# First products in blocks of 512 tokens two batches behind the attention, x carried through memory in float32, thirteen float32 pairs instead of nine

## The chip, the cores and the metric

The kernel runs on one core of a Trainium2 chip. The core has a matrix engine (TensorE, called PE in the rows; its weight loads are PEld), VectorE (DVE), ScalarE (ACT), GpSimd (POOL) and SyncE (SP), which here only issues DMAs. The metric is the device time of one execution in microseconds; lower is better. Arrays are prepared on the host before the launch (q and k are transposed, the weights are handed over as pairs of 32-bit words), and everything after that is on the core.

## The reference

Weights are float64 in the input; they reach the kernel as two 32-bit words each and are decoded to float32 on the chip. What is computed, with B = 8 batches, H = 12 heads, S = 448, D = 64, d_model 768, d_ff 1024:

```
scores = (1/sqrt(64)) * q @ k^T - log(448)
attn   = 1 / (1 + exp(-scores))
x      = (attn @ v) as [3584 tokens, 768]
a = x @ w1 ;  b = x @ w2
out = ((a * b) @ w3) @ w_out          # float32
```

## The kernel before

Two heads make a pair: 6 pairs in a batch, 48 in all. A pair is worked in 4 **slots**, one for each chunk of keys (three of 128, one of 64), so there are 192 slots, 24 in a batch. In slot s PE does the scores of that chunk, then the attention product (`av`) of the slot before; between them ACT makes the sigmoids.

There are two kinds of pair. The first `PLAIN` = 9 pairs (slots 0 to 35) are **plain**: float32 matmuls on float32 operands (tiles `qp`, `ap`, `vv`; lines 203 and 255), which cost PE more but need no splitting. The other 39 split each operand into a float32r high part and a rest (`qs`, `kh`, `kl`, `vs`, `ah`, `al`; lines 206, 232 and 262), which costs DVE, ACT and POOL work. The first split pair needs tiles of a pool `pf` that takes the room of the pool `pp` for early weights, so its q and k are loaded at the pair before it (`prepare`, line 399).

A pair's result is 128 columns of x (one of NK = 6 chunks, `kc`) for the 448 tokens of its batch. `combine` (line 267) splits it into `xh` and `xl`, the operands of the **first products**, on ACT and DVE. The first products, `up` (line 330), multiply x by w1 and w2, each product as three float32r matmuls (high by high, high by rest, rest by high): 8 column chunks x 2 weights x 6 chunks x 3 = 288 matmuls for a block of tokens. They go between the slots' scores and `av`, 12 in a slot (`ups`, line 418), one batch behind: the block of batch b-1 goes into the slots of batch b. The blocks take turns at 384 and 512 tokens: an even batch leaves its last 64 tokens (`CARRY`) as split parts in memory (`x_dram`), and the odd batch after it reads them back ahead of its own 448. The seventh block ends after the last slot, and the eighth (512 tokens) is done in the tail. The product a*b (`g`) of each column chunk goes to memory (`g_dram`, line 352).

Weights are decoded by DVE in six instructions for a job (lines 93 to 109), after ACT has made the magnitude (line 86); then ACT casts the high part and DVE subtracts it (lines 73 and 74). w1 and w2 are 16 jobs of 128 x 768, w3 16 jobs of 128 x 512 that go to memory. `starts` and `steps` (lines 366 to 369) say in which slot each step stands: eight w1/w2 jobs in slots 1 to 22, the other eight in slots 25 to 35, while first products already run; the w3 jobs stand in every pair of batches 2, 4 and 6. The first 13 jobs (`EARLY`) have three buffers for the raw words (pool `pp`), the rest one (pool `pd`).

The order on PE and SP is the order in which the code is written (`manual_schedule`, line 362); up to slot 31 the same holds for ACT and POOL. DVE's order, and later ACT's, is chosen by the scheduler. Every engine works its own queue strictly in order.

After the slots comes the tail: the last block of first products with w_out decoded beside it, then w3 times w_out (line 593), then the last product in blocks of two batches (line 626).

Of the kernel before, what the change touches and what calls it, by code (L numbers as in the profile page):

```python
# [11 lines left out]
F32 = mybir.dt.float32  # L12
F32R = mybir.dt.float32r
# [12 lines left out]
def sigmoid_attention_bilinear_ffn(  # L26
# [20 lines left out]
    P = 128  # L47
# [16 lines left out]
    phase_d, phase_s = ExitStack(), ExitStack()  # L64
    pd = phase_d.enter_context(tc.tile_pool(name="pd", bufs=2))
# [3 lines left out]
    x_dram = dram.tile([NK, P, 2, CARRY], F32, name="x_dram")  # L69
# [6 lines left out]
    def load_words(src, pool=None):  # L76
        if pool is None:
            raw = pd.tile([P, NK, P, 2], U32, name="raw", bufs=1)[:, :src.shape[1]]
        else:
            raw = pool.tile([P, *src.shape[1:-1], 2], U32, name="raw")  # L80
        nc.sync.dma_start(out=raw, in_=src)
        return raw

    def magnitude(raw):
        f = pd.tile([P, *raw.shape[1:-1]], F32, name="f")
        nc.scalar.activation(f, raw[..., 1].bitcast(F32), AF.Abs, scale=HW_SCALE)  # L86
        return f
# [29 lines left out]
    px0 = phase_a.enter_context(tc.tile_pool(name="px0", bufs=NK, side="right"))  # L117
    pa = phase_a.enter_context(tc.tile_pool(name="pa", bufs=2, side="right"))
    px = (px0, px1)
# [107 lines left out]
    def short_scores(ks, qs):  # L227


        sp = ps.tile([P, 2, 512], F32, name="sp", bufs=2)[:, :, :S]  # L230
        for j in range(2):
            nc.tensor.matmul(sp[:, j], ks[:, j], qs[:, j], start=True, stop=True)  # L232
        t = pf[0].tile([P, S], F32, name="st", bufs=1)
        add_halves(t, [sp[:, j] for j in range(2)])
        return t
# [31 lines left out]
    def combine(b, kc, accs):  # L267
        if len(accs) == 1:
            src = accs[0][:, :S]
        else:  # L270
            src = pm.tile([P, S], F32, name="t", bufs=1)
            add_halves(src, [acc[:, :S] for acc in accs])
        second = b % 2
        n = BLOCKS[second]
        xh = px[second].tile([P, n], F32R, name="xh")
        xl = px[second].tile([P, n], F32R, name="xl")
        if second:
            for i, x in enumerate((xh, xl)):
                nc.sync.dma_start(out=x[:, :CARRY].bitcast(F32), in_=x_dram[kc, :, i])
            split(xh[:, CARRY:], xl[:, CARRY:], src, nc.scalar.copy, nc.vector)  # L280
        else:
# [24 lines left out]
    def load_job(i):  # L306
        _, _, cs, src = jobs[i]
        raws[i] = load_words(src[:, cs], pp) if i < EARLY else load_words(src[:, cs])

    def decode_weights():  # L310

        for i, (n, at, cs, _) in enumerate(jobs):
            if i + 2 < EARLY:
                load_job(i + 2)
            for k in (i, i + 1):
                if k not in fs and k in raws:
                    fs[k] = magnitude(raws[k])
            f = decode(raws.pop(i), fs.pop(i))
            if i + 1 >= EARLY and i + 1 < len(jobs):
                load_job(i + 1)  # L320
            if n == 3:
                nc.sync.dma_start(out=w3_dram[at, :, cs], in_=f)
                yield
                continue
            yield
            half, at = divmod(at, NH)
            split(wh[n][half][:, at, cs], wl[n][half][:, at, cs], f, nc.scalar.copy, nc.vector)
            yield

    def up(b, xs, banks, pool, bufs):  # L330

        n_t = BLOCKS[b % 2]
        at_t = b // 2 * 2 * S + b % 2 * BLOCKS[0]
        for fc in range(NF):
            for n in (1, 2):
                acc = pool.tile([P, 512], F32, name="up", tag=next(banks), bufs=bufs)
                for kc in range(NK):
                    xh, xl = xs[kc]
                    for m, (w, x) in enumerate(((wh[n], xh), (wh[n], xl), (wl[n], xh))):
                        nc.tensor.matmul(  # L340
                            acc[:, :n_t], w[fc // NH][:, fc % NH, kc], x,
                            start=(kc == 0 and m == 0), stop=(kc == NK - 1 and m == 2),
                        )
                        if (kc, m) != (NK - 1, 2):
                            yield
                if n == 1:
                    a_sb = pm.tile([P, BLOCKS[1]], F32, name="a_sb", bufs=1)[:, :n_t]
                    nc.scalar.copy(out=a_sb, in_=acc[:, :n_t])
                    yield
            g = pm.tile([P, BLOCKS[1]], F32, name="g", bufs=1)[:, :n_t]  # L350
            nc.vector.tensor_tensor(out=g, in0=acc[:, :n_t], in1=a_sb, op=ALU.mult)
            nc.sync.dma_start(out=g_dram[fc, :, at_t:at_t + n_t], in_=g)
            yield

# [10 lines left out]
    first = NPAIR * NC  # L365
    starts = [1 + 3 * i for i in range(8)] + [first + 1 + 3 * i // 2 for i in range(8)]
    assert len(starts) == 2 * NF
    later = [p * NC + 1 for p, (b, _) in enumerate(pairs) if b > 1 and b % 2 == 0][:2 * NF]
    steps = starts + [s + 2 - s // first for s in starts] + later

    EARLY = sum(s < (PLAIN - 1) * NC for s in starts)
    qks, vvs = {}, {}
    for p in range(2):
# [6 lines left out]
    xs = {b: [] for b in range(B)}  # L380
    filler = iter(())
# [4 lines left out]
    def attend_due(slot):  # L386
        while waiting and waiting[0][0] <= slot:
            _, p, c, ops = waiting.pop(0)
            if c == 0:
                accs[p] = [  # L390
                    ps.tile([P, 512], F32, name="av", bufs=2) for _ in range(1 if p < PLAIN else 2)
                ]
            attend(c, ops, vs[p], accs[p])
            if c == NC - 2:
                b, kc = pairs[p]
                xs[b].append(combine(b, kc, accs.pop(p)))
                del vs[p]
# [18 lines left out]

    chunks = [0, NC - 1, *range(1, NC - 1)]
    ups = -(-(NF * 2 * NK * 3) // (NPAIR * NC))
    slot = 0
    for p, (b, hp) in enumerate(pairs):  # L420
# [4 lines left out]
        if p == PLAIN - 1:  # L425
            phase_p.close()
            pf.append(phase_a.enter_context(tc.tile_pool(name="pf", bufs=2, side="right")))
        qs, kh, kl, ks = splits.pop(p)
        for i, c in enumerate(chunks):
            prepare(p, i)  # L430
# [23 lines left out]
    p3 = phase_w.enter_context(tc.tile_pool(name="p3", bufs=2, side="right"))  # L454
    woh = p3.tile([P, NF, DM], F32R, name="woh", bufs=1)
# [10 lines left out]
    filler = up(B - 1, xs[B - 1], itertools.repeat("acc"), ps2, 8)  # L466
    for jc in range(NF):
        take(filler, 10)
        for half in range(2):
            ms = slice(half * NM, (half + 1) * NM)  # L470
            src = w_out[jc * P:(jc + 1) * P].rearrange("p (m u) -> p m u", u=2)[:, ms]
            raw = load_words(src, p3)
            f = decode(raw, magnitude(raw))
            split(woh[:, jc, ms], wol[:, jc, ms], f, nc.scalar.copy, nc.vector)
    ics = [c + NH * h for c in range(NH) for h in range(2)]
    w3s = {0: w3_chunk(0)}
    take(filler, 10 ** 6)
    phase_x.close()
    phase_d.close()
# [228 lines left out]
```

## Time and profile before

| what | value |
|---|---|
| median of 3 runs | 1094.63 us (1092.42 to 1095.91) |
| the profiled execution | 1092.5 us |
| its span, first to last instruction | 1090.3 us |
| mean granted TensorE clock | 0.986 of full speed |
| PE busy | 1054.4 us, 97% |
| DVE busy | 820.0 us, 75% |
| ACT busy | 614.4 us, 56% |
| moved by DMA | 150.69 MB, 138 GB/s on the mean |

The span runs from the first to the last instruction, and the profiled execution took 2.2 us more than its span. Busy shares are means over stages that have different limits, so the table alone does not say what a change is worth: the stages have to be looked at one by one.

### The profile page before, as it was taken

What the parts mean: (1) busy time and instruction counts of PE and PEld (TensorE: products, weight loads), DVE (VectorE), ACT (ScalarE), POOL (GpSimd) and SP (SyncE); (2) the same over time, 40 slices, a digit from 0 to 9 for tenths busy, and PEclk for the clock granted to TensorE, in tenths of its full rate; (3) what the DMA queues carried; (4) which work ended last, traced back from release to release, by engine and by line L of the source; (5) the groups of instructions that cost most, each with busy time, mean ns of one, the idle gap of its engine ahead of it and who ended that gap; (6) DMA issues with size and microseconds to landing.
All of it is one profiled execution on the core that took longest, in us unless ns stands there. A gap on an engine that the chain in (4) does not pass through costs nothing.

```text
span 1090.3 us, 14870 instructions
## 1 busy us (share of the span) xinstructions
PE 1054.4 (97%) x5076; PEld 902.9 (83%) x5076; DVE 820.0 (75%) x1335; ACT 614.4 (56%) x937; POOL 183.6 (17%) x277
## 2 busy tenths in 40 slices
PE   7899689999999999999999999999999999999998
PEld 1245579888899988789998889998889999999997
DVE  6778778788787877887787866867875767868672
ACT  5664557667677766667776667774325442424230
POOL 0001042223332221333322323310000000000000
PEclk9899889999999999999999999999999999999999
DMA  8574444455444444444444443324433735657452
GB/s 247 167 208 118 113 112 114 122 142 144 108 108 121 116 131 133 124 121 116 115 123 116 139 112 104 87 63 127 142 113 109 261 116 200 228 188 223 159 163 76
DMA packets 119002, 150.69 MB, mean 138 GB/s; under 512 B 16336, under 2 KB 104592, under 8 KB 118928
## 3 DMA queue, kind: packets, MB, share of 16 engines
q1 hardware_dynamic: 118928, 149.76, 47.0%
q8 instruction: 40, 0.66, 0.3%
q14 instruction: 34, 0.28, 0.1%
HBM read 118.26 MB, written 31.46 MB: 137 GB/s over the span
## 4 chain that ended last, share of the span: by engine, by line
PE 71%; DVE 14%; DMA 6%; ACT 3%; issue 3%; SPq 2%; POOL 1%; DVEq 0%; ACTq 0%; POOLq 0%
PE up L340 30%; PE up L626 19%; PE av L262 8%; PE sp L206 7%; PE up L593 5%; DMA qq<-qT 2%; DMA raw<-w3T 2%; DVE al L224 2%; DMA raw<-w 1%; DVE raw L106 1%; ACT f L86 1%; DVE f L101 1%; DVE t L194 1%; PE sp L232 1%; DVE w L74 1%
## 5 line engine op out<-in xcount | busy, mean ns | idle before, releaser
L340 PE MATMUL up<-xh,w 128*128 128x384 f32 (+1 forms) x1536 | 466.3, 367 | 0.7 <-issue 0.7
L340 PEld LDWEIGHTS up<-xh,w 128*128 128x128 f32 x1536 | 287.7, 189 | 39.6 <-issue 6.9
L340 PE MATMUL up<-xl,w 128*128 128x384 f32 (+1 forms) x768 | 282.1, 367 | 0.0
L187 ACT ACTIVATE ah<-sp,bias 128x896 fp32r<-128x896 f32 x117 | 117.9, 1008 | 83.1 <-PE sp L206 82.3
L340 PEld LDWEIGHTS up<-xl,w 128*128 128x128 f32 x768 | 145.3, 189 | 15.0
L224 DVE TENSOR_TENSOR al<-sp,ah 128x896 fp32r<-128x896 f32 x117 | 127.4, 1089 | 30.0 <-ACT sp L187 28.3
L74 POOL TENSOR_TENSOR kl<-kk,kh 128x896 fp32r<-128x896 f32 x39 | 83.8, 2148 | 392.1 <-DVE kh L73 350.8
L626 PE MATMUL up<-gs,w 128*128 128x448 f32 x576 | 119.3, 367 | 0.0
L626 PEld LDWEIGHTS up<-gs,w 128*128 128x128 f32 x576 | 108.1, 188 | 9.9
L187 ACT ACTIVATE sp<-sp,bias 128x896 f32<-128x896 f32 x117 | 113.7, 971 | 0.0
L262 PE MATMUL av<-ah,vs 128*128 128x448 f32 x312 | 103.7, 372 | 6.0 <-DVE t L194 3.9
L262 PE MATMUL av<-al,vs 128*128 128x448 f32 x234 | 87.2, 373 | 5.1 <-DVE al L224 4.8
L206 PE MATMUL sp<-qs,kh 128*128 128x448 f32 x234 | 87.4, 374 | 4.5 <-DVE kh L73 4.5
L626 PE MATMUL up<-ga,w 128*128 128x448 f32 x432 | 89.5, 366 | 0.0
L206 PE MATMUL sp<-qs,kl 128*128 128x448 f32 x234 | 87.4, 373 | 1.7 <-POOL kl L74 1.7
L74 POOL TENSOR_TENSOR vs<-vv,vs 128x256 fp32r<-128x256 f32 x78 | 62.5, 814 | 147.4 <-DVE vs L73 144.9
L626 PEld LDWEIGHTS up<-ga,w 128*128 128x128 f32 x432 | 81.1, 188 | 7.1
L246 DVE TENSOR_TENSOR ah<-st,ah 64x448 fp32r<-64x448 f32 x78 | 52.1, 668 | 45.2 <-ACT st L187 43.8
L86 ACT ACTIVATE f<-raw 128x768 f32<-128x768 f32 (+2 forms) x48 | 34.1, 710 | 77.3 <-DMA raw<-w3T 25.0
L262 PEld LDWEIGHTS av<-ah,vs 128*128 128x128 f32 x312 | 58.5, 188 | 16.3 <-issue 8.5
L73 ACT CAST ga<-graw 128x448 fp32r<-128x448 f32 x48 | 25.8, 566 | 70.1 <-DMA graw<-g_dram 70.1
L193 ACT COPY t<-av 64x448 f32<-64x448 f32 x78 | 41.2, 528 | 33.7 <-PE av L262 32.7
(74 smaller groups left out, 1519.8 us busy)
## 6 DMA issues: line engine op xcount, KB each, us to landing
graw<-g_dram SPq DMA_DIRECT2D x72, 448.0 KB, 4.4
qq<-qT SPq DMA_DIRECT2D x78, 224.0 KB, 4.0
kk<-kT SPq DMA_DIRECT2D x78, 224.0 KB, 4.5
raw<-w SPq DMA_DIRECT2D x16, 768.0 KB, 5.7
vv<-vL SPq DMA_DIRECT2D x48, 192.0 KB, 2.6
raw<-w3T SPq DMA_DIRECT2D x16, 512.0 KB, 4.4
g_dram<-g SPq DMA_DIRECT2D x32, 256.0 KB, 2.2
g_dram<-g SPq DMA_DIRECT2D x32, 192.0 KB, 1.9
```

The lines of the kernel that those rows point to most:

```text
L73: hi_engine(out=dst_hi, in_=src)
L74: lo_engine.tensor_tensor(out=dst_lo, in0=src, in1=dst_hi, op=ALU.subtract)
L86: nc.scalar.activation(f, raw[..., 1].bitcast(F32), AF.Abs, scale=HW_SCALE)
L187: nc.scalar.activation(dst, src, AF.Sigmoid, bias=bias[:n], scale=scale)
L193: nc.scalar.copy(out=dst[rows], in_=src[j][others])
L206: nc.tensor.matmul(sp[:, j], k[:, j, at:at + n], qs[:, j], start=m == 0, stop=m == 1)
L224: nc.vector.tensor_tensor(out=al, in0=sp, in1=ah, op=ALU.subtract)
L246: nc.vector.tensor_tensor(out=a[others, j], in0=t[rows], in1=a[rows, j], op=ALU.subtract)
L262: nc.tensor.matmul(accs[j][:, :S], v[:, c, j].rearrange("p u d -> p (u d)"), a[:, j], start=first and m == 0, stop=last and m == len(ops) - 1,
L340: nc.tensor.matmul(acc[:, :n_t], w[fc // NH][:, fc % NH, kc], x, start=(kc == 0 and m == 0), stop=(kc == NK - 1 and m == 2),)
L593: nc.tensor.matmul(acc[:, :NM], a[:, jc], w[:, jc, ms], start=(jc == 0 and m == 0), stop=(jc == NF - 1 and m == 2),)
L626: nc.tensor.matmul(acc[:, :TB], w[:, c, ms], g[:, c], start=(c, m) == (0, 0), stop=(c, m) == (NH - 1, 2),)
```

## The change

- x goes through memory whole, in float32. `combine` leaves a float32 tile `t` (an ACT copy in a plain pair, the sum of two halves in a split one); `store_x` writes it a slot later, `load_x` reads 512 tokens of one chunk two slots after that (`xr`), and `split_x` splits them in the slot after the load.
- First products go in 7 blocks of 512 tokens instead of 8 of 384 and 512, so 2016 matmuls instead of 2304. They begin at slot 53 (`BEGIN`) and no longer at slot 26, with 12 in a slot as before; 60 of them are left after the last slot, and the seventh block is in the tail.
- `PLAIN` is 13: slots 0 to 51 are plain, 35 pairs are split.
- All 16 w1/w2 jobs stand in slots 1 to 45, one in every 2.75 slots, all with three buffers; the magnitude of the next job stands two slots after a job's decoding and the split of its own three slots after. The w3 jobs stand in every second pair from the 14th pair on, with their loads one job ahead.
- Each `g` is stored seven matmuls after it was asked of DVE (`late`), and no longer at once.
- Sixteen matmuls on zeros stand ahead of the first scores.
- The raw words of w_out get a pool of their own in the tail.

```diff
-    CARRY = 64
-    BLOCKS = (S - CARRY, S + CARRY)
-    PLAIN = 9
+    TU = 512
+    NU = NT // TU
+    PLAIN = 2 * NPAIR + 1
...
-    x_dram = dram.tile([NK, P, 2, CARRY], F32, name="x_dram")
+    x_dram = dram.tile([NK, P, NT], F32, name="x_dram")
...
-    px1 = phase_x.enter_context(tc.tile_pool(name="px1", bufs=NK, side="left"))
+    px = phase_x.enter_context(tc.tile_pool(name="px", bufs=2 * NK - 1, side="left"))
...
     def combine(b, kc, accs):
+        t = pa.tile([P, S], F32, name="t")
         if len(accs) == 1:
-            src = accs[0][:, :S]
+            nc.scalar.copy(out=t, in_=accs[0][:, :S])
         else:
-            src = pm.tile([P, S], F32, name="t", bufs=1)
-            add_halves(src, [acc[:, :S] for acc in accs])
-        second = b % 2
-        n = BLOCKS[second]
-        xh = px[second].tile([P, n], F32R, name="xh")
-        xl = px[second].tile([P, n], F32R, name="xl")
-        if second:
-            for i, x in enumerate((xh, xl)):
-                nc.sync.dma_start(out=x[:, :CARRY].bitcast(F32), in_=x_dram[kc, :, i])
-            split(xh[:, CARRY:], xl[:, CARRY:], src, nc.scalar.copy, nc.vector)
-        else:
-            split(xh, xl, src[:, :n], nc.scalar.copy, nc.vector)
-            xt = pm.tile([P, 2, CARRY], F32R, name="xt")
-            split(xt[:, 0], xt[:, 1], src[:, n:], nc.scalar.copy, nc.vector)
-            nc.sync.dma_start(out=x_dram[kc], in_=xt.bitcast(F32))
+            add_halves(t, [acc[:, :S] for acc in accs])
+        return t
+
+    def store_x(b, kc, t):
+        nc.sync.dma_start(out=x_dram[kc, :, b * S:(b + 1) * S], in_=t)
+
+    def load_x(n, kc):
+        xr = pm.tile([P, TU], F32, name="xr")
+        nc.sync.dma_start(out=xr, in_=x_dram[kc, :, n * TU:(n + 1) * TU])
+        return xr
+
+    def split_x(xr):
+        xh = px.tile([P, TU], F32R, name="xh")
+        xl = px.tile([P, TU], F32R, name="xl")
+        split(xh, xl, xr, nc.scalar.copy, nc.vector)
         return xh, xl
...
+                        if late is not None and (n, kc, m) == (1, 2, 0):
+                            nc.sync.dma_start(out=g_dram[late[0], :, at_t:at_t + TU], in_=late[1])
+                            late = None
...
-    starts = [1 + 3 * i for i in range(8)] + [first + 1 + 3 * i // 2 for i in range(8)]
-    later = [p * NC + 1 for p, (b, _) in enumerate(pairs) if b > 1 and b % 2 == 0][:2 * NF]
-    EARLY = sum(s < (PLAIN - 1) * NC for s in starts)
+    starts = [1 + 11 * i // 4 + k for i in range(2 * NF) for k in (0, 2, 3)]
+    later = [p * NC + 1 for p in range(PLAIN + 1, len(pairs), 2)][:2 * NF]
+    EARLY = 2 * NF
+    PER = NPAIR * NC
+    BEGIN = 2 * PER + NC + 1
...
+    warm = ps.tile([P, 512], F32, name="up", tag="up", bufs=2)
+    for _ in range(16):
+        nc.tensor.matmul(warm[:, :S], zeros[:, :P], zeros, start=True, stop=True)
...
-    filler = iter(())
+    filler = itertools.chain(*(up(n, xs[n], itertools.repeat("up"), ps, 2) for n in range(NU - 1)))
...
+    def x_due(slot):
+        for at in [k for k in xts if (k[0] * NPAIR + k[1] + 1) * NC < slot]:
+            store_x(*at, xts.pop(at))
+        for n in range(NU):
+            for kc in range(NK):
+                at = (n + 1) * PER + (kc + 1) * NC + 3
+                if slot == at:
+                    xrs[n, kc] = load_x(n, kc)
+                if slot == at + 1:
+                    xs[n].append(split_x(xrs.pop((n, kc))))
...
-            if b > 0 and (hp, i) == (0, 2):
-                take(filler, 10 ** 6)
-                filler = up(b - 1, xs[b - 1], itertools.repeat("up"), ps, 2)
-            take(filler, ups)
+            x_due(slot)
+            if slot >= BEGIN:
+                take(filler, ups)
...
+    for at in range(slot, slot + NC + 1):
+        x_due(at)
     take(filler, 10 ** 6)
...
-    filler = up(B - 1, xs[B - 1], itertools.repeat("acc"), ps2, 8)
+    filler = up(NU - 1, xs[NU - 1], itertools.repeat("acc"), ps2, 8)
```

How this moves instructions is shown at three places. The first is ACT at the end of the second plain pair, where its order is the written one. Before, `xh` and `xt` are casts of the attention result `av`, and `ap` the sigmoid of a slot:

```order
L187 ACTIVATE ap<-sp,bias 128x896
L73 CAST xh<-av 128x384
L73 CAST xt<-av 128x64
L187 ACTIVATE ap<-sp,bias 64x896
L73 CAST w<-f 128x768
L187 ACTIVATE ap<-sp,bias 128x896
L86 ACTIVATE f<-raw 128x768
```

Now, at the same place, with `t` the float32 copy of the pair's result:

```order
L184 ACTIVATE ap<-sp,bias 128x896 x2
L83 ACTIVATE f<-raw 128x768
L267 COPY t<-av 128x448
L184 ACTIVATE ap<-sp,bias 64x896
L73 CAST w<-f 128x768
L184 ACTIVATE ap<-sp,bias 128x896 x2
```

The two casts, the second of which stands behind a subtraction on DVE, have given way to one copy, and the cast of x is now taken from a reloaded tile in later slots.

The second place is PE at the first split pair. Before, 12 first products (`up`) already stand in each of the slots around it:

```order
L255 MATMUL av<-ap,vv 64x448 x2
L206 MATMUL sp<-qs,kh 128x448
L206 MATMUL sp<-qs,kl 128x448
L206 MATMUL sp<-qs,kh 128x448
L206 MATMUL sp<-qs,kl 128x448
L340 MATMUL up<-xh,w 128x384
L340 MATMUL up<-xl,w 128x384
```

Now the plain slots run up to it bare, and the first products begin one slot later:

```order
L252 MATMUL av<-ap,vv 64x448 x2
L203 MATMUL sp<-qs,kh 128x448
L203 MATMUL sp<-qs,kl 128x448
L203 MATMUL sp<-qs,kh 128x448
L203 MATMUL sp<-qs,kl 128x448
L252 MATMUL av<-ap,vv 64x448 x2
L229 MATMUL sp<-qs,ks 128x448 x2
L347 MATMUL up<-xh,w 128x512
L347 MATMUL up<-xl,w 128x512
```

So the whole of slots 0 to 52 has no first products beside it.

The third place is the queue of SP in a pair among the split ones. Before, the stores of `g` and of the carried tokens `xt` stand right behind the work that makes them:

```order
L352 DMA g_dram<-g 128x512
L285 DMA x_dram<-xt 128x128
L151 DMA vv<-vL 128x3x128
L155 DMA vv<-vL 64x128 x2
L81 DMA raw<-w3T 128x4x256
L322 DMA w_dram<-f 128x512
L142 DMA qq<-qT 64x2x448 x2
L142 DMA kk<-kT 64x2x448 x2
```

Now, for a pair of the same kind:

```order
L273 DMA x_dram<-t 128x448
L139 DMA qq<-qT 64x2x448 x2
L139 DMA kk<-kT 64x2x448 x2
L277 DMA xr<-x_dram 128x512
L352 DMA g_dram<-g 128x512
L148 DMA vv<-vL 128x3x128
L152 DMA vv<-vL 64x128 x2
```

Each pair has gained a store of 224 KB and a load of 256 KB, the loads of q and k stand between the two, and the store of `g` has moved behind them.

## Rows read from the trace of the kernel before

**Rows 1.** Part 1 of the page: busy us (share of the span) xinstructions.

```profile
PE 1054.4 (97%) x5076; PEld 902.9 (83%) x5076; DVE 820.0 (75%) x1335; ACT 614.4 (56%) x937; POOL 183.6 (17%) x277
```

**Rows 2.** Four stages: us; busy PE, PEld, DVE, ACT, POOL (count); PEclk; DMA; GB/s.

```profile
0.00:66.30 66.30, 55.38 (x205) 13.66 (x205) 47.68 (x71) 41.72 (x55) 0.20 (x4) 0.92 0.68 211
66.30:162.00 95.70, 81.12 (x374) 60.48 (x373) 74.21 (x105) 47.60 (x65) 16.47 (x22) 0.91 0.47 126
162.00:746.40 584.40, 578.95 (x2822) 519.10 (x2821) 458.19 (x708) 410.80 (x602) 166.95 (x252) 1.00 0.43 116
746.40:1090.30 343.90, 338.91 (x1680) 309.64 (x1680) 239.92 (x452) 114.32 (x216) 0.00 (x0) 1.00 0.51 166
```

**Rows 3.** PE in order of time, early: start us, us, instruction [idle before <-releaser].

```profile
4.17 3.55 PE L203 MATMUL sp<-qp 64*128 64x448 f32 x8 [4.17 <-DMA qp<-kT]
...
29.45 1.02 PE L203 MATMUL sp<-qp 64*128 64x448 f32 x4
...
31.30 1.02 PE L203 MATMUL sp<-qp 64*128 64x448 f32 x4
...
40.32 1.76 PE L255 MATMUL av<-ap,vv 64*64 64x448 f32 x4 [2.48 <-ACT ap L187]
...
83.66 1.02 PE L203 MATMUL sp<-qp 64*128 64x448 f32 x4
...
87.83 1.02 PE L203 MATMUL sp<-qp 64*128 64x448 f32 x4
```

**Rows 4.** ACT in order of time, two places; columns as in rows 3.

```profile
39.16 0.21 ACT L73 CAST xt<-av 128x64 fp32r<-128x64 f32 x1 [2.82 <-DVE xl L74]
...
118.70 0.89 ACT L86 ACTIVATE f<-raw 128x768 f32<-128x768 f32 x1 [3.38 <-DMA raw<-w]
```

**Rows 5.** The chain that ended last: start us, us, what.

```profile
512.34 2.12 PE up L340 x12
...
526.58 2.12 PE up L340 x12
...
587.34 2.75 PE up L340 x12
...
604.12 2.75 PE up L340 x12
...
746.38 65.57 PE up L340 x288
```

**Rows 6.** PE behind an idle stretch; columns as in rows 3.

```profile
124.08 0.57 PE L206 MATMUL sp<-qs,kh 128*128 128x448 f32 x1
124.45 0.57 PE L206 MATMUL sp<-qs,kl 128*128 128x448 f32 x1
```

**Rows 7.** DVE in order of time, decoding; columns as in rows 3.

```profile
13.59 0.95 DVE L109 TENSOR_TENSOR f<-f,raw 128x768 f32<-128x768 f32 x1
...
66.33 0.96 DVE L109 TENSOR_TENSOR f<-f,raw 128x768 f32<-128x768 f32 x1
...
82.99 0.56 DVE L93 TENSOR_SCALAR raw<-raw 128x768 uint32<-128x768 uint32 x1
83.46 0.55 DVE L351 TENSOR_TENSOR g<-up,a_sb 128x384 f32<-128x384 f32 x1
...
84.39 0.62 DVE L74 TENSOR_TENSOR xl<-av,xh 128x448 fp32r<-128x448 f32 x1
...
89.33 0.56 DVE L93 TENSOR_SCALAR raw<-raw 128x768 uint32<-128x768 uint32 x1
```

**Rows 8.** Waits of SP's queue, whole span: us in total, times, longest us.

```profile
SPq L352 <- DVE g L351: 271.4, 48, 11.2
SPq L285 <- DVE xt L74: 155.9, 24, 11.9
```

**Rows 9.** Part 6 of the page: issues, KB each, median us to landing.

```profile
kk<-kT SPq DMA_DIRECT2D x78, 224.0 KB, 4.5
...
g_dram<-g SPq DMA_DIRECT2D x32, 256.0 KB, 2.2
```

More of the change, by code (lines that the diff above doesn't have):

```diff
@@ L307, in load_job, with load_magnitude @@
         _, _, cs, src = jobs[i]
-        raws[i] = load_words(src[:, cs], pp) if i < EARLY else load_words(src[:, cs])
+        raws[i] = load_words(src[:, cs], *((pp, 3) if i < EARLY else (pd, 1)))
+    def load_magnitude(i):
+        fs[i] = magnitude(raws[i], *((pp, 3) if i < EARLY else (pd, 2)))
     def decode_weights():
         for i, (n, at, cs, _) in enumerate(jobs):
[L313 to L322, printed above, removed]
+            if i < EARLY:
+                if i == 0:
+                    load_magnitude(0)
+                if i + 2 < EARLY:
+                    load_job(i + 2)
+                f = decode(raws.pop(i), fs.pop(i))
+                yield
+                if i + 1 < EARLY:
+                    load_magnitude(i + 1)
+                else:
+                    load_job(i + 1)
+                yield
+                half, at = divmod(at, NH)
+                split(wh[n][half][:, at, cs], wl[n][half][:, at, cs], f, nc.scalar.copy, nc.vector)
                 yield
                 continue
-            yield
-            half, at = divmod(at, NH)
-            split(wh[n][half][:, at, cs], wl[n][half][:, at, cs], f, nc.scalar.copy, nc.vector)
+            load_magnitude(i)
+            f = decode(raws.pop(i), fs.pop(i))
+            if i + 1 < len(jobs):
+                load_job(i + 1)
+            nc.sync.dma_start(out=w3_dram[at, :, cs], in_=f)
             yield
     def up(b, xs, banks, pool, bufs):
-        n_t = BLOCKS[b % 2]
-        at_t = b // 2 * 2 * S + b % 2 * BLOCKS[0]
+        at_t = b * TU
+        late = None
         for fc in range(NF):
@@ L346, in up @@
                 if n == 1:
-                    a_sb = pm.tile([P, BLOCKS[1]], F32, name="a_sb", bufs=1)[:, :n_t]
-                    nc.scalar.copy(out=a_sb, in_=acc[:, :n_t])
+                    a_sb = pm.tile([P, TU], F32, name="a_sb", bufs=1)
+                    nc.scalar.copy(out=a_sb, in_=acc)
                     yield
-            g = pm.tile([P, BLOCKS[1]], F32, name="g", bufs=1)[:, :n_t]
-            nc.vector.tensor_tensor(out=g, in0=acc[:, :n_t], in1=a_sb, op=ALU.mult)
-            nc.sync.dma_start(out=g_dram[fc, :, at_t:at_t + n_t], in_=g)
+            g = pm.tile([P, TU], F32, name="g", bufs=1)
+            nc.vector.tensor_tensor(out=g, in0=acc, in1=a_sb, op=ALU.mult)
+            late = fc, g
             yield
+        nc.sync.dma_start(out=g_dram[late[0], :, at_t:at_t + TU], in_=late[1])
     def take(stream, n):
@@ L363, in sigmoid_attention_bilinear_ffn @@
     pairs = [(b, hp) for b in range(B) for hp in range(NPAIR)]
-    first = NPAIR * NC
-    starts = [1 + 3 * i for i in range(8)] + [first + 1 + 3 * i // 2 for i in range(8)]
-    assert len(starts) == 2 * NF
-    later = [p * NC + 1 for p, (b, _) in enumerate(pairs) if b > 1 and b % 2 == 0][:2 * NF]
-    steps = starts + [s + 2 - s // first for s in starts] + later
-    EARLY = sum(s < (PLAIN - 1) * NC for s in starts)
+    starts = [1 + 11 * i // 4 + k for i in range(2 * NF) for k in (0, 2, 3)]
+    later = [p * NC + 1 for p in range(PLAIN + 1, len(pairs), 2)][:2 * NF]
+    assert len(later) == 2 * NF
+    steps = starts + later
+    EARLY = 2 * NF
+    PER = NPAIR * NC
+    BEGIN = 2 * PER + NC + 1
     qks, vvs = {}, {}
+    zeros = pp.tile([P, S], F32R, name="zeros", bufs=1)
+    nc.vector.memset(zeros.bitcast(U32), 0)
     for p in range(2):
@@ L377, in sigmoid_attention_bilinear_ffn @@
             vvs[0] = load_v(*pairs[0])
+    warm = ps.tile([P, 512], F32, name="up", tag="up", bufs=2)
+    for _ in range(16):
+        nc.tensor.matmul(warm[:, :S], zeros[:, :P], zeros, start=True, stop=True)
     splits, vs = {0: split_pair(0 < PLAIN, *qks.pop(0))}, {0: split_v(0 < PLAIN, vvs.pop(0))}
     weights = decode_weights()
-    xs = {b: [] for b in range(B)}
-    filler = iter(())
+    xs = {n: [] for n in range(NU)}
+    xts, xrs = {}, {}
+    filler = itertools.chain(*(up(n, xs[n], itertools.repeat("up"), ps, 2) for n in range(NU - 1)))
     waiting = []
@@ L454, in sigmoid_attention_bilinear_ffn @@
     p3 = phase_w.enter_context(tc.tile_pool(name="p3", bufs=2, side="right"))
+    phase_r = ExitStack()
+    pr = phase_r.enter_context(tc.tile_pool(name="pr", bufs=2, side="right"))
     woh = p3.tile([P, NF, DM], F32R, name="woh", bufs=1)
@@ L471, in sigmoid_attention_bilinear_ffn @@
             src = w_out[jc * P:(jc + 1) * P].rearrange("p (m u) -> p m u", u=2)[:, ms]
-            raw = load_words(src, p3)
-            f = decode(raw, magnitude(raw))
+            raw = load_words(src, pr, 2)
+            f = decode(raw, magnitude(raw, pr, 2))
             split(woh[:, jc, ms], wol[:, jc, ms], f, nc.scalar.copy, nc.vector)
```

35 lines of the change are left out of this document (16 added, 19 removed).

## The prediction

> **What bounds the kernel now.** I read the page's busy times first, then cut the span into stages, then went into the stages that lose time. PE is busy 97% of the span [rows 1], so a gain can only come from fewer or quicker matmuls or from the 3% of idle time and the stretches at the lower clock. The stage table [rows 2] says where these are. The cuts are my own: 66.3 us is the scores of slot 26, the first slot with first products; 162 us is about slot 45; 746.4 us is the first matmul of the tail. From 162 us on PE is idle for 5.5 of 584.4 us and, in the tail, for 5 of 343.9, at a clock of 1.00. Ahead of that it is idle for 10.9 of 66.3 us and 14.6 of 95.7, and the clock there is 0.92 and 0.91. The reader is to see that the loss sits in the first 162 us.
>
> How much it is needs the length of a slot on undisturbed PE. A plain slot is 31.30 - 29.45 = 1.85 us [rows 3]. Four slots of a split pair with 48 first products of 384 columns are 526.58 - 512.34 = 14.24 us, with 512 columns 604.12 - 587.34 = 16.78 us; twelve first products of 384 take 2.12 us (0.177 each), and the 288 of 512 in the tail 65.57 us (0.228 each) [rows 5]. A plain slot with twelve of 384 is 87.83 - 83.66 = 4.17 us [rows 3], 0.2 more than its parts. Slots 0 to 25 would be 26 x 1.85 = 48 us and took 66.3: 18 lost. Slots 26 to 44 (ten plain with twelve products, 4.17; nine split, 14.24 / 4) would be 73.7 and took 95.7: 22 lost. So the first 162 us lose about 40 us and the rest of the slots 5.5.
>
> Two mechanisms of the loss are seen. At a pair's end ACT's cast `xt` waits 2.82 us for a subtraction that stands behind decoding on DVE; the sigmoid behind it is late, PE idles 2.48 us, and four matmuls then take 1.76 us [rows 3, 4]. Around the first split pair ACT's magnitude waits 3.38 us for the raw words, which have one buffer there [rows 4]; afterwards matmuls of 448 columns follow each other every 0.37 us [rows 6], which is the 1.2 GHz level.
>
> **The change part by part.** I lay out the new slots in order and add up the end.
>
> *Slots 0 to 52.* Three engines run neck and neck. PE needs 53 x 1.85 = 98 us. DVE has 16 jobs: from one job's first instruction to the next one's is 89.33 - 82.99 = 6.34 us, with a `g` of 0.55 and an `xl` of 0.62 in between, so 5.2 us a job where nothing waits [rows 7]; I take 5.3. A job stands in every 2.75 slots, 5.1 us of PE, so DVE sets the pace by a little. ACT has a sigmoid in each slot, a magnitude and a cast for each job and a copy for each pair; it waits for DVE only at the cast `w`, since the copy `t` reads PE's result alone. The wait of 2.82 us has gone with `xt`.
>
> The start: sixteen zeros matmuls at 0.37 us [rows 6] take 6 us from about 1.4 us on, to 7.4, where the first scores began at 4.17 [rows 3]. PE is in-order, so the first scores, the first sigmoids and with them the first magnitude on ACT are some 2.5 us later; against that the next scores run at the higher clock. I price it as the first job ending near 17 us instead of 14.5 [rows 7]. Without any gain of the clock it is 3 us, and at best -2. Fifteen more jobs are 15 x 5.3 = 79.5, and four splits of x fall among them (0.62 for 448 columns, so 0.7 for 512): 2.8. The last job ends at 99.3, its cast lets slot 46 begin at 101; slots 46 to 51 are 6 x 1.85 and slot 52 about 1.7 (four split scores, one plain `av`): 114. The first split pair's k can be asked for only when the scores of slot 47 are done, at about 105; issue about 1, landing 4.5 [rows 9], then a cast on DVE and a subtraction on POOL, about 113 to 114: it fits within a microsecond. I add 3 us for that and for short falls of the clock: slot 53 begins at **117**. Bounds: PE alone, 7.4 + 98 = 105.5; the old pace of jobs, (66.33 - 13.59) / 8 = 6.6 us over the eight jobs that ran without first products [rows 7], adds 15 x 1.3 = 19.5: 136.5. I take the value near the undisturbed row, because what disturbed the old pace (`xt`, one raw buffer) is what goes.
>
> *Slots 53 to 191.* First products 12 a slot, all 512: 34 pairs x 16.78 and three slots, 16.78 - 4.4: 582.9. What remains behind the last slot is 60 x 0.228 = 13.7, and the last `av` about 1.2: **597.8** together. In this the edits cancel on PE: 1728 products of 0.228 are 393.5 us where 1152 of 0.177 and 864 of 0.228 were 400.4; four more plain pairs cost 4 x 7.4 = 29.6 and save four split ones, 4 x (14.24 - 8.48) = 23. That is 0.3 us less; 27 slots fewer in which PE changes between products and attention save those 0.2 each, 5.
>
> One page of the Trainium skill would make the first of these numbers smaller. By the rows a product of 384 columns costs 0.0167 us above its columns at 2.4 GHz and one of 512 0.0144, so fewer and longer ones save 6.9 us. "TensorE: Matmul & The Clock Gate", section "Back-to-back issue gap", gives columns over 2.4 GHz and 2.5 ns; by that the saving is 0.8 us and the sum 6 us higher. The rows differ from the page, and I keep the rows.
>
> *Stalls among these slots.* Before, 5.5 us idle and some at the lower clock. The w3 jobs now come every 33 us and no longer every 17 in bursts. SP waited 271.4 us in total for `g` and 155.9 for `xt` [rows 8], with the loads of the next pair queued behind; both stores now stand after their work is done. New on SP: a store and a load a pair. The store waits for `t`, made in the slot before, and the loads of q, k and v stand behind it; the load waits for the store. Their way is 0.35 + 2.2 (as `g`, 256 KB), 0.4 + 4.5 (as `kk`, 224 KB) [rows 9], the subtraction 0.7 and ACT's cast taken as long: 8.9 us, hidden by first products of five slots, 5.25 x 4.2 = 22 us from the store's turn to the product that needs the last chunk. I put the stalls at **4**; bounds 0 and 12.
>
> *Tail.* The same 288 products, then the same work: 343.9 [rows 2]. The last x comes back behind 60 products, 13.7 us against 8.9. Bounds -2 and +4.
>
> Sum: 117 + 597.8 + 4 + 343.9 + 2.2 around the span = 1064.9, against this execution's 1092.5: 27.6 less. The median shown is 2.1 above that execution, so the forecast is **1067 us**. Cross-check by losses: 40 + 5.5 were lost, 19 (117 - 98) and 4 will be, and 5 are saved on changes between kinds of work.
>
> **The rivals.**
>
> *The old pace stays.* DVE's order is the scheduler's, ACT's casts stand in line with the sigmoids, and DVE and PE are within 4% of each other, so each handshake shows. Then slot 53 comes at 136.5 and the time is 1086 or 1087. For it: DVE was busy 47.7 of the first 66.3 us and still set the pace [rows 2]. Against it: `xt`.
>
> *DMA sets the first stage.* Words (12.6 MB), 13 pairs' q, k, v (9), x out and back (4), the rest (1.4) are 27 MB in slots 0 to 52. The first stage moved 211 GB/s at a busy share of 0.68 [rows 2], so full engines would do about 310, and 27 MB need 87 us of the 117. Should the loads come no faster than that 211, it is 128 us plus the start, slot 53 at about 132, and 1082. "DMA: Bandwidth & Descriptors", section "Specifications", has a limit of about 358 GB/s for a core, by which 27 MB are an estimated 75 us; page and row agree that it is no floor here.
>
> *x comes back late (slower).* The new round trip goes through SP, in order. If SP holds the store and the load each by as much as its longest waits before, 11.9 us [rows 8], the trip is 8.9 + 23.8 = 32.7 against the 22 of cover: 10.7 us in each of six blocks, 64 us, time 1131. It decides from 13 us of hold on; to end slower than before it takes about 18. Against it: what held SP is gone or earlier.
>
> *It does not do what it says.* The zeros matmuls may end before the clock rises; that is inside the bounds of the start.
>
> **How the numbers follow.** The forecast 0.71, with its own range 1053 to 1080; old pace 0.14; DMA 0.07; x late 0.08, of which I leave 0.02 to times within the noise. 0.3%, some 3.3 us, is about what a measurement of this kernel can tell from no change. Faster 0.88, same 0.05 (0.03 of it from the old pace with the upper bound of stalls), slower 0.07 (0.06 by late x, 0.01 by the old pace with stalls and tail both at their upper ends). The range for 8 in 10 reaches from 1051 to 1089.
>
> **What would show it.** A first stage in which PE is nearly bare of idle stretches over 1 us, ACT's `w` waiting briefly for DVE and no other wait of ACT above 1 us; the first `up` at 112 to 122 us; pairs 16.8 us apart behind it; SP's waits for DVE down from 430 us by more than half. I am wrong if the first `up` comes after 130 us, if the raw words land later than the magnitude wants them, or if PE idles at every 24th slot for `xl`.

## The result and the profile after

The changed kernel took 1066.62 us (median of 4, 1061.42 to 1069.40) against 1095.27 for the kernel before (median of 4): ratio 0.9735, 95% interval 0.9686 to 0.9783. The forecast was 1067. The profiled execution took 1068.97 us, its span 1067.2, so of the forecast's sum of 1064.9 it is 4.1 us off; that the medians agree to half a microsecond is partly luck, since the four runs are 8 us apart and the errors of the terms below partly cancel.

These are the stages of the changed kernel, cut at about slot 27, at slot 53 and at the tail; columns as in [rows 2], to which they answer:

```profile
0.00:57.69 57.69, 54.62 (x228) 17.26 (x228) 46.38 (x65) 43.61 (x52) 0.20 (x4) 1.00 0.86 268
57.69:120.88 63.19, 54.45 (x211) 13.88 (x209) 46.45 (x68) 42.59 (x54) 4.19 (x7) 0.89 0.65 198
120.88:719.97 599.09, 597.94 (x2707) 507.37 (x2705) 467.45 (x680) 398.14 (x563) 159.84 (x238) 1.00 0.50 142
719.97:1067.20 347.23, 340.49 (x1680) 311.22 (x1680) 231.45 (x433) 109.25 (x208) 0.00 (x0) 1.00 0.48 157
```

Slots 53 to 191 have PE idle for 1.2 us of 599. The first 57.69 us are close to PE's own pace: 27 slots from 7.04 us on are 50.65 us, 1.88 each against 1.85. They are at DVE's pace as well: from the second decoding to the twelfth (the first instructions of these jobs are shown, columns as in [rows 7]) ten jobs take 52.81 us, 5.28 each. From 10.83 to 73.54 us DVE is busy for 61.43 of 62.71 us.

```profile
15.40 0.55 DVE L90 TENSOR_SCALAR raw<-raw 128x768 uint32<-128x768 uint32 x1
68.21 0.55 DVE L90 TENSOR_SCALAR raw<-raw 128x768 uint32<-128x768 uint32 x1
```

The next 63.19 us hold 26 slots, 48.1 us at PE's pace; 15 us are lost there, at a clock of 0.89.

| term | forecast | profile |
|---|---|---|
| slot 53 begins | 117 | 120.9 |
| slots 53 to 191, the 60 products, the last `av`, stalls | 597.8 + 4 | 599.1 |
| tail | 343.9 | 347.2 |
| around the span | 2.2 | 1.8 |

The chain of waits of the changed kernel (start us, us, what) answers to [rows 5] and shows what stood on the path:

```profile
1.42 5.70 PE up L394 x16
64.65 4.54 DMA x_dram<-t
69.20 4.56 DMA xr<-x_dram
84.61 4.55 DMA x_dram<-t
97.13 3.82 DMA raw<-w3T
252.41 2.75 PE up L347 x12
269.18 2.75 PE up L347 x12
719.97 65.56 PE up L347 x288
819.75 6.28 DMA graw<-g_dram
828.70 5.79 DMA graw<-g_dram
```

A pair is 269.18 - 252.41 = 16.77 us, as before. But three kinds of DMA now stand on the path ahead of slot 53, none of which the forecast had there: stores of x, the loads that wait for them, and the first words of w3. ACT in the changed kernel shows what they do (columns as in [rows 4], idle before in brackets):

```profile
73.79 0.62 ACT L73 CAST xh<-xr 128x512 fp32r<-128x512 f32 x1 [3.63 <-DMA xr<-x_dram]
100.97 0.66 ACT L83 ACTIVATE f<-raw 128x512 f32<-128x512 f32 x1 [3.78 <-DMA raw<-w3T]
```

PE stands still behind the first of them and then runs at the lower level (1.2 GHz) for a while (columns as in [rows 3]); the same four matmuls take 0.97 us at the upper one. The last line is PE behind the second wait, where the granted clock is 0.59 from 100 to 110 us:

```profile
70.78 0.97 PE L252 MATMUL av<-ap,vv 128*64 128x448 f32 x4
71.68 1.02 PE L200 MATMUL sp<-qp 64*128 64x448 f32 x4
75.79 0.97 PE L252 MATMUL av<-ap,vv 64*64 64x448 f32 x4 [3.09 <-ACT ap L184]
76.69 1.02 PE L200 MATMUL sp<-qp 64*128 64x448 f32 x4
77.64 1.57 PE L252 MATMUL av<-ap,vv 128*64 128x448 f32 x4
79.14 1.86 PE L200 MATMUL sp<-qp 64*128 64x448 f32 x4
...
102.58 1.76 PE L252 MATMUL av<-ap,vv 128*64 128x448 f32 x4 [3.10 <-ACT ap L184]
```

SP's longest waits, in answer to [rows 8] (us in total, times, longest us):

```profile
SPq L273 <- DVE t L191: 214.1, 35, 10.8
SPq L352 <- DVE g L361: 146.3, 30, 8.0
...
SPq L277 <- DMA x_dram<-t: 18.1, 9, 4.1
```

### The profile page after: what moved, and what is told of

The parts are those of the page before. It is cut to its first block, busy times and chain, and to the rows that moved or that the text cites. A ratio compares the mean times of both kernels' runs of the same rounds, so it can differ in the third digit from the quotient of the medians.

```text
span 1067.2 us, 14185 instructions
## 1 busy us (share of the span) xinstructions
PE 1047.5 (98%) x4820; PEld 849.7 (80%) x4820; DVE 791.7 (74%) x1242; ACT 593.6 (56%) x876; POOL 164.2 (15%) x249
## 4 chain that ended last, share of the span: by engine, by line
PE 87%; DVE 5%; DMA 4%; ACT 1%; issue 1%; SPq 0%; ACTq 0%; DVEq 0%
PE up L347 42%; PE up L658 19%; PE av L259 10%; PE sp L203 8%; PE up L625 5%; PE sp L229 1%; DMA graw<-g_dram 1%; DMA x_dram<-t 1%; DVE f L98 1%; DVE raw L103 1%; PE sp L200 1%; PE av L252 1%; DVE w L74 1%; DMA xr<-x_dram 1%; DVE raw L90 1%
## 5 line engine op out<-in xcount | busy, mean ns | idle before, releaser
L347 PE MATMUL up<-xh,w 128*128 128x512 f32 x1344 | 438.9, 391 | 1.1 <-ACT f L83 1.1
L347 PEld LDWEIGHTS up<-xh,w 128*128 128x128 f32 x1344 | 252.3, 188 | 54.5 <-ACT f L83 1.5
L347 PE MATMUL up<-xl,w 128*128 128x512 f32 x672 | 263.1, 392 | 0.0
L184 ACT ACTIVATE ah<-sp,bias 128x896 fp32r<-128x896 f32 x105 | 105.7, 1006 | 111.3 <-PE sp L203 111.3
L221 DVE TENSOR_TENSOR al<-sp,ah 128x896 fp32r<-128x896 f32 x105 | 114.4, 1090 | 62.8 <-ACT sp L184 62.1
L347 PEld LDWEIGHTS up<-xl,w 128*128 128x128 f32 x672 | 126.2, 188 | 23.2
L184 ACT ACTIVATE sp<-sp,bias 128x896 f32<-128x896 f32 x105 | 101.9, 970 | 0.0
L259 PE MATMUL av<-ah,vs 128*128 128x448 f32 x280 | 92.0, 369 | 0.0
L252 PE MATMUL av<-ap,vv 128*64 128x448 f32 (+1 forms) x208 | 53.6, 595 | 10.4 <-ACT ap L184 10.4
L184 ACT ACTIVATE ap<-sp,bias 128x896 f32<-128x896 f32 (+1 forms) x52 | 51.8, 1004 | 19.3 <-PE sp L200 19.2
```

The lines of the kernel that those rows point to most:

```text
L184: nc.scalar.activation(dst, src, AF.Sigmoid, bias=bias[:n], scale=scale)
L221: nc.vector.tensor_tensor(out=al, in0=sp, in1=ah, op=ALU.subtract)
L252: nc.tensor.matmul(accs[0][cols, :S], v[:ops[0].shape[0], c, cols], ops[0][:, j], start=first, stop=last,)
L259: nc.tensor.matmul(accs[j][:, :S], v[:, c, j].rearrange("p u d -> p (u d)"), a[:, j], start=first and m == 0, stop=last and m == len(ops) - 1,
L347: nc.tensor.matmul(acc[:, :TU], w[fc // NH][:, fc % NH, kc], x, start=(kc == 0 and m == 0), stop=(kc == NK - 1 and m == 2),)
```

## The experiments

Ratios are to the kernel before, timed on the same chip in the same job; only they are compared between jobs, because the chips differ by some microseconds. "First product" is the start of the first `up` in the profiled execution, 121.4 us in the changed kernel.

**1. The splits of the first block's x one slot later.**

```diff
-                if slot == at + 1:
+                if slot == at + (2 if n == 0 else 1):
```

> The changed kernel with the split of each reloaded x chunk of the first block (slots 32 to 52) one slot later, so that ACT meets the cast 1.85 us later. Theory A (what the first stage still loses over PE's own pace is ACT waiting for DMA, here 3.63 us at one reload and about 2 at two others, with the lower clock after it): the stretch of slots 27 to 44 gets 4 to 6 us shorter and the time falls to about 1062. Theory B (DVE's decoding sets the pace of the stage, as the forecast had it): the wait only moves from the DMA to DVE, time within 1 us of 1066.6. Theory C (DMA is full in this stage): the reload lands as much later as it is asked for, no change either, and the wait stays at the same cast.

Ratio 0.9731 (0.9698 to 0.9765), first product at 115.4 us. At the reload that cost 3.63 us ACT now waits 0.92. The words of w3 still hold it:

```profile
74.12 0.62 ACT L73 CAST xh<-xr 128x512 fp32r<-128x512 f32 x1 [0.92 <-DMA xr<-x_dram]
97.78 0.66 ACT L83 ACTIVATE f<-raw 128x512 f32<-128x512 f32 x1 [4.77 <-DMA raw<-w3T]
```

The trace goes with theory A: slots 27 to 44 take 36.3 us instead of 40.8, and the first product comes 6 us earlier. The ratio does not resolve it: its interval is as wide as the effect.

**2. The first w3 words at slot 53.**

```diff
-                else:
-                    load_job(i + 1)
...
+            if i == EARLY:
+                load_job(i)
+                yield
...
-    steps = starts + later
+    steps = starts + [2 * NPAIR * NC + NC + 1] + later
```

> The changed kernel with the load of the first w3 words moved from slot 44 to slot 53, so that its magnitude, which the scheduler set ahead of the sigmoids of slots 44 to 47, stands behind slot 53. Theory A (ACT's 3.78 us wait for these words and the half clock behind it cost slots 45 to 48 some 7.6 us): the first products begin near 114 and no longer at 121 us, time about 1060. Theory B (DVE sets the pace; 3.4 us of decoding only move to a place with room): 3 us less, about 1063. If the wait for k of the first split pair takes its place: no change.

Ratio 0.9755 (0.9720 to 0.9790), first product at 117.6 us. That wait is gone, and a reload takes most of its place, so the first product stays short of theory A's 114:

```profile
73.53 0.62 ACT L73 CAST xh<-xr 128x512 fp32r<-128x512 f32 x1 [3.70 <-DMA xr<-x_dram]
105.60 0.62 ACT L73 CAST xh<-xr 128x512 fp32r<-128x512 f32 x1 [2.84 <-DMA xr<-x_dram]
```

**3. Both.**

> Both of the delays together: the splits of the first block's x one slot later, and the first w3 words asked for at slot 53. Theory A: the two waits are independent and add up, first products at 108 to 111 us, time 1055 to 1058, and DVE's busy share up to slot 52 rises over 80%. Theory B (decoding sets the pace): 3 us at most, about 1063. Theory C (DMA full): the words of w1 and w2 land late in their place, about 1064.

Ratio 0.9721 (0.9688 to 0.9753), first product at 115.2, where theory A had 108 to 111: hardly earlier than with the first delay alone. They do not add up. The cast of a late chunk waits in place of the words:

```profile
103.20 0.62 ACT L73 CAST xh<-xr 128x512 fp32r<-128x512 f32 x1 [4.05 <-DMA xr<-x_dram]
```

**4. No zeros.** Without the sixteen matmuls and their memset.

> The changed kernel without the sixteen matmuls on zeros and their memset. By the forecast's own bounds the zeros cost 3 us without any gain of the clock and give 2 at best. By the traces: the scores of slot 2 stand at 10.07 us with them and at 10.27 in the kernel before, slot 3 at 11.93 and 13.12, so they should be worth 0 to 1.5 us: time 1066 to 1069. If the clock's level at the start decides a later fall of the clock too, more than 3 us slower.

Ratio 0.9747 (0.9715 to 0.9778), first product at 122.1. The scores of slot 2 begin at 11.2 us against 10.07 with zeros. Worth about a microsecond in the trace, nothing in the ratio, as the bounds had it.

**5. The kernel before, with a copy ahead of the casts.**

```diff
-            src = accs[0][:, :S]
+            src = pm.tile([P, S], F32, name="t", bufs=1)
+            nc.scalar.copy(out=src, in_=accs[0][:, :S])
```

> The kernel before with one edit: a plain pair's result is copied by ACT into a float32 tile, and the casts xh and xt read that copy and no longer PE's result. Theory A (the wait of ACT's xt for DVE at each pair's end, the idle PE and the lower clock behind it, are a good part of the 18 us lost in slots 0 to 25): the scores of slot 26 begin near 58 us and no longer at 66.3, time 7 to 9 us below the kernel before (ratio 0.992). Theory B (decoding at DVE's pace sets the stage): the copy costs ACT 0.5 us a pair and gives nothing, ratio 1.000 to 1.004. Should the order of ACT and not the tile be what makes xt wait, no change either.

Ratio 0.9978 (0.9959 to 0.9997), 2.4 us. The waits of `xt` are gone, yet slot 26 still begins at 66.40 us. ACT waits at the magnitudes now, for a buffer (`w` is the subtraction that frees it) or for the words:

```profile
32.38 0.89 ACT L86 ACTIVATE f<-raw 128x768 f32<-128x768 f32 x1 [1.50 <-DVE w L74]
46.80 0.89 ACT L86 ACTIVATE f<-raw 128x768 f32<-128x768 f32 x1 [3.07 <-DMA raw<-w]
```

Theory A falls for this stage. `xt` was the wait that came last, with another close behind it.

**6. The kernel before, with thirteen plain pairs.**

```diff
-    PLAIN = 9
+    PLAIN = 13
```

> The kernel before with thirteen plain pairs and no other edit; with it all sixteen jobs of w1 and w2 get three buffers, and the first split pair stands at slot 52, long behind the last job. Theory A (some 18 of the 22 us lost in slots 26 to 44 are the collision of the first split pair with jobs whose words have one buffer): they go, four more plain pairs cost PE 6.6 us, time 8 to 12 us below the kernel before (ratio 0.990). Theory B (it is the first products beside the decoding that lose the time): the loss stays and the plain pairs come on top, 4 to 7 us above (ratio 1.005).

Ratio 0.9874 (0.9846 to 0.9901), 13.8 us, though PE has 6.6 us more to do. The two stages of this run up to 170 us:

```profile
0.00:68.20 68.20, 56.25 (x209) 13.94 (x209) 48.68 (x73) 41.86 (x55) 0.20 (x4) 0.92 0.66 205
68.20:170.00 101.80, 101.61 (x490) 62.41 (x489) 52.75 (x80) 44.57 (x58) 4.24 (x7) 1.00 0.41 124
```

PE is now idle for 0.2 us of 101.8, with first products and half of the decoding side by side. Theory A holds here, and theory B (products beside decoding lose the time) is refuted. The one edit does two things, though: it moves the split pairs away from the decoding, and it gives the last three jobs three buffers for their words. Which of the two brought the gain was not tried.

**7. The kernel before, with both edits.**

> Both edits on the kernel before: the copy and thirteen plain pairs. Theory A: 15 to 20 us below the kernel before (ratio 0.984), which leaves 9 to 13 us of the whole change to what is not in it: first products two batches behind, blocks of 512, w3 in every second pair, later stores. Theory B: no change.

Ratio 0.9860 (0.9831 to 0.9890). The copy adds nothing that can be told; slot 26 begins at 66.63 us.

**8. Each g stored at once.**

```diff
-                        if late is not None and (n, kc, m) == (1, 2, 0):
-                            nc.sync.dma_start(out=g_dram[late[0], :, at_t:at_t + TU], in_=late[1])
-                            late = None
...
-            late = fc, g
+            nc.sync.dma_start(out=g_dram[fc, :, at_t:at_t + TU], in_=g)
...
-        nc.sync.dma_start(out=g_dram[late[0], :, at_t:at_t + TU], in_=late[1])
```

> The changed kernel with each g stored on SP right behind its product, as before the change, and no longer seven matmuls later. Theory A (SP's long waits for g cost nothing, since the loads behind them are asked for pairs ahead): time within 1.5 us of the changed kernel, ratio to the kernel before as there, 0.97 to 0.975. Theory C (the split slots lost their 5.5 us and more to loads queued behind these waits): 4 to 6 us slower, ratio 0.978, with PE idle at the starts of blocks.

Ratio 0.9752 (0.9721 to 0.9782). SP again waits 247.8 us for `g`, and PE is idle for 1.9 of 598 us among the split slots, against 0.2 in the same stretch of the changed kernel:

```profile
121.00:719.00 598.00, 596.14 (x2694) 504.99 (x2693) 463.73 (x674) 395.63 (x560) 167.39 (x238) 1.00 0.51 141
```

The later store is not where the gain is: SP waits some 90 us longer for `g` and 100 us less for `t` (114.4 us), and PE's idle time differs by 1.7 us.

**9. The kernel before, with both edits and the change's steps for a job.** The magnitude of the next job two slots after a job's decoding, its own split three after (1 and 2 for the second eight jobs):

```diff
+            if i < EARLY:
...
+                f = decode(raws.pop(i), fs.pop(i))
+                yield
+                if i + 1 < EARLY:
+                    fs[i + 1] = magnitude(raws[i + 1])
...
-    steps = starts + [s + 2 - s // first for s in starts] + later
+    steps = [s + k for s in starts for k in ((0, 2, 3) if s < first else (0, 1, 2))] + later
```

> The kernel before with the copy and thirteen plain pairs (as the run with both edits) and, in addition, the change's three steps for a w1 or w2 job: the next job's magnitude two slots after a job's decoding and its own split three slots after, where the magnitude stood beside the decoding and the split two slots after. Theory D (formed on the last runs: the 18 us lost in slots 0 to 25 are ACT meeting magnitudes whose words or buffers are not there yet, and casts whose decoding is not done; with the copy the wait only went from xt to the magnitudes): the scores of slot 26 come at 54 to 58 us and no longer at 66.4, time 8 to 11 us below the run with both edits, ratio 0.977. Theory B (DVE's pace): no change, ratio 0.986.

Ratio 0.9779 (0.9756 to 0.9802), 8.9 us below experiment 7; slot 26 begins at 56.93. Its stages:

```profile
0.00:58.00 58.00, 51.47 (x209) 13.08 (x210) 45.35 (x71) 45.10 (x62) 0.20 (x4) 1.00 0.78 239
58.00:170.00 112.00, 112.00 (x534) 68.75 (x536) 60.85 (x90) 52.08 (x68) 7.06 (x12) 1.00 0.41 121
```

The work of experiment 6's first stage is done in 10 us less. DVE had been kept waiting there: in experiment 7 it is busy for 40.85 of 49.29 us from 13.71 on, and a job takes 7.04 us; here for 48.56 of 49.46 us from 16.54 on, and a job takes 5.59. These three edits hold 24 of the 29 us, with first products still from slot 26 on and blocks of 384 and 512. For everything else in the change, the larger blocks, their later start and x in memory among it, 5 us are left; these were not taken apart.

**10. The changed kernel with the old steps.**

```diff
-    starts = [1 + 11 * i // 4 + k for i in range(2 * NF) for k in (0, 2, 3)]
+    starts = [1 + 11 * i // 4 + k for i in range(2 * NF) for k in (0, 0, 2)]
```

> The changed kernel with the steps of a job placed as before the change: the next job's magnitude beside a job's decoding, its own split two slots after. Theory D: slots 0 to 45 lose again what they lost before, 0.5 to 0.8 us a job on the mean, first products near 130 us, 8 to 12 us slower than the changed kernel, ratio 0.981 to 0.985. Theory B: no change, ratio 0.9735.

Ratio 0.9733 (0.9710 to 0.9757), first product at 121.5: no change. Theory D in that form fails on this kernel. ACT waits 2.02 and 2.37 us at the first two jobs and under 0.9 at any later w1/w2 job, where experiment 5 waited at most jobs. Slot 26 begins 2.4 us later than in the changed kernel, and none of that is left at the first product. DVE is not kept waiting: from 20.96 to 69.20 us it is busy for 47.10 of 48.24 us.

```profile
12.82 0.89 ACT L83 ACTIVATE f<-raw 128x768 f32<-128x768 f32 x1 [2.02 <-DMA raw<-w]
17.88 0.83 ACT L73 CAST w<-f 128x768 fp32r<-128x768 f32 x1 [2.37 <-DVE f L106]
```

The changed kernel has a third buffer for the magnitudes, which the kernel before has not, and no store of `xt` in SP's queue ahead of the words. Either would explain why the place of the steps decides in one kernel and not in the other; neither was tried alone.

**11. w3 in bursts.**

```diff
-    later = [p * NC + 1 for p in range(PLAIN + 1, len(pairs), 2)][:2 * NF]
+    later = [p * NC + 1 for p, (b, _) in enumerate(pairs) if p > PLAIN and b % 2 == 0][:2 * NF]
+    later += [p * NC + 1 for p, (b, _) in enumerate(pairs) if b == 7][:2 * NF - len(later)]
```

> The changed kernel with the w3 jobs in every pair of batches 2, 4 and 6, as before the change (16 of them, from the 15th pair on). Theory E (DVE runs full where a w3 job comes every 17 us, and PE idled there for 5.5 us): 3 to 6 us slower, ratio 0.977 to 0.979, with idle PE behind the bursts. Theory F (the split slots lost time only through the carried tokens and the loads queued behind them): no change.

Ratio 0.9759 (0.9727 to 0.9790): not told from the changed kernel. PE is idle for 2.1 of 598 us, against 0.2 in the same stretch of the changed kernel. Theory E is not borne out; the spacing of w3 is worth some 2 us.

**12. The waits taken out as far as they were known.** Experiment 2's edit and

```diff
-                if slot == at + 1:
+                if slot == at + (1 if n else 2 if kc == NK - 1 else 3):
```

> A version that should beat both kernels: the changed kernel with the first block's reloaded x split two slots later than in the change (one for its last chunk), and the first w3 words asked for at slot 53. Theory A (what is left over PE's pace up to slot 52 is ACT waiting for DMA, and with enough slack nothing takes its place): first products at 109 to 112 us, time 6 to 8 us below the changed kernel, ratio 0.967. Theory C (DMA, which moved 268 GB/s at a share of 0.86 in slots 0 to 26, is the floor): 115 us as in the run with both delays, ratio 0.972.

Ratio 0.9683 (0.9659 to 0.9707), 1060.24 us: the lowest of all. Against the changed kernel's 0.9735 the intervals overlap. But experiment 10, which has the changed kernel's ratio, ran in the same job on the same chip and took 1064.71 to 1066.48 us, and this version took 1058.62 to 1061.04: it is very likely the faster one. The first product comes 7 us earlier than in the changed kernel, at 114.3. That is near theory C's 115 and not theory A's 109 to 112, but DMA, at a share of 0.73 in the second stage, was not full there. DVE is busy for 83.79 of the 85.43 us from 10.87 to 96.30, so up to slot 46 DVE has no time left to give. Its two early stages and the longest wait for a DMA that is left ahead of slot 53:

```profile
0.00:57.70 57.70, 54.64 (x228) 17.28 (x229) 46.36 (x65) 43.55 (x52) 0.20 (x4) 1.00 0.86 268
57.70:113.00 55.30, 49.07 (x208) 12.87 (x208) 43.41 (x62) 42.37 (x52) 4.32 (x7) 0.97 0.73 220
```

```profile
102.33 0.62 ACT L73 CAST xh<-xr 128x512 fp32r<-128x512 f32 x1 [3.77 <-DMA xr<-x_dram]
```

That cast is written for slot 50 and stands in ACT's queue ahead of the sigmoid of slot 47. The written order of ACT ends at slot 48, and what is written behind it is placed by the scheduler. The w3 magnitude of slot 57 got ahead of the sigmoid of slot 44 in the same way.

## Why the prediction was right, and where not

*What bounds the kernel.* Right: most of the gain lies ahead of slot 53. All that stands before the tail's first product fell from 746.4 to 720.0 us, 26.4 less, and the tail gave 3.3 of it back. Of what was lost over PE's pace, 40 us ahead of slot 45 became 120.9 - 98 = 23 ahead of slot 53. DMA was not the floor of the first stage: it moved 268 GB/s there at a share of 0.86, and PE was idle for 3.1 us of 57.7.

*Slots 26 to 44 of the kernel before.* Right in place and size: 22 us were lost there, and experiment 6 gives some 20 back, less 6.6 for the plain pairs. That the collision of the split pairs with words in one buffer was the cause fits; its two halves were not tried apart.

*Slots 0 to 25.* The step that failed is "the wait of 2.82 us has gone with `xt`" as a price. Experiment 5 took that wait away and gained 2.4 us of the 18; the next wait, at the magnitudes, was as long. Experiment 9 let slot 26 begin 9.7 us earlier than experiment 7 by the places of a job's steps alone, to which the forecast gave no price. What goes with them is the time for which DVE is kept waiting, 8.4 us of 49.3 against 0.9 of 49.5.

*"DVE sets the pace by a little."* Right, almost to the figure: a job takes 5.28 us where 5.3 was taken, against 5.16 for 2.75 slots of PE, and DVE runs without a gap. PE feels it now and then: ACT waits 0.25 to 0.78 us for DVE at seven of the ten casts `w` up to 63 us, and PE idles 0.70, 0.75 and 0.81 us at 17.30, 38.41 and 59.52. The last job ended at 100.07 us, where the forecast had 99.3; that is partly luck, since the first ended at 15.5 instead of 17 and DVE stood idle for 3.9 us between 73.54 and 100.07.

*"It waits for DVE only at the cast w".* Incomplete, and it cost most of the 3.9 us by which this term was short. Slot 46 began 4.2 us after the last job's end and not 1.7, because ACT waited for the words of w3; slots 46 to 52, the first of them at the lower clock, took 16.6 us where 12.8 and the 3 added stood. That the words land later than the magnitude wants them was a sign of being wrong by the prediction's own list, and two waits of ACT for DMA were far above the 1 us that it allowed. The round trip of x was priced in split slots of 4.2 us, where it is hidden as forecast (the stage of 599 us), but the first block's chunks come back in plain slots. From the store's turn to the cast there are three slots, 5.6 us; store and load took 4.54 + 4.56 us where 2.2 + 4.5 stood in the sum, and even those would not have fitted. The rival of a late x was thus there, in another place and at about a tenth of its price. Experiments 1 to 3 show that these waits stand close behind each other: two delays together gave no more than one.

*Slots 53 to 191.* 599.1 against 601.8. The stalls forecast at 4 were 1.2. Without the later stores (8) or without the spacing of w3 (11) PE idles for 1.7 or 1.9 us more, so each may be a part of the 5.5 us that went and neither is all of it; x whole instead of carried tokens, and equal blocks, were not tried. SP's waits for DVE at the stores of x and `g` fell from 427 to 372 us and not by half, as the prediction wanted to see; 214 of them now stand at the store of x, and PE is idle for only 1.2 us in the whole stretch.

*Fewer and longer products.* The rows' price held: 288 products of 512 columns took 65.56 us, 0.228 each. The formula that the prediction set beside it says nothing against it: in the Trainium skill, "TensorE: Matmul & The Clock Gate", section "Back-to-back issue gap", it is the gap of an isolated matmul, and these stand in a stream. Its 2.5 ns for 288 products fewer are an estimated 0.7 us, not 0.8.

*Tail.* 3.3 us longer, inside the bounds given. Of that, 1.3 us are in the 20 us that hold the two loads of `g` in the chain, and 1.6 in the 94 matmuls behind them (18.14 us, 16.57 before), which begin at a granted clock of 0.55 (838.7 to 842.0 us; 1.00 at that place before). Why the chain waits longer there was not tried.

## What to carry to other kernels

Where a stage has several waits on one in-order engine, the one that the trace names is only the last to end: taking it away is worth the distance to the next, which an experiment gives and a trace does not. A round trip through memory is to be checked against the shortest slots that it crosses, with the landing times of that stage's DMA load, and not against the usual ones. What an engine does in the rest of its time matters more than its busy share: DVE was kept waiting for 17% of the early stage, and other places for a job's steps, which added no work, took that away and brought 8.9 us. Moving two kinds of work that collide apart can be worth more than the extra work it costs: four plain pairs, and the buffers that came with them, cost PE 6.6 us and brought 13.8 net.

## What the runs showed of the hardware

The same transfer can take more than twice its median to land: 224 KB to memory landed in 4.54 us at 64.65 us of the changed kernel, while DMA moved 264 GB/s at a share of 0.81, in 1.91 us at 103.49, at 120 GB/s and 0.33, and in 2.0 on the median of its 48. The share alone does not tell the time: at 84.61 us it was 4.55 us at 0.68, at 74.86 us 2.07 at 0.65. The sixteen matmuls on zeros had the clock at its upper level by 7.04 us: the first eight score matmuls took 1.92 us, 3.55 without [rows 3].
